# Slot-table fills paced by half head over the attention stage of a bucketed-attention and two-MoE kernel

## The chip, the core and the metric

One core of one Trainium2 chip runs the whole program. The metric is the device time of one execution in microseconds (us); lower is better. Inside the core TensorE (PE in the profile, its weight loads PEld), VectorE (DVE), ScalarE (ACT) and GpSimd (POOL) compute; SyncE (SP) issues most transfers, and sixteen DMA engines carry them. Each engine runs its own instructions strictly in the order in which they stand in its queue, and waits where an instruction waits.

## What is computed

Three layers in a row: attention inside hash buckets, then a mixture of experts with one expert per token, then one with two experts per token. Cut to what matters:

```python
# attention: 2 batches x 8 heads = 16 heads, 768 tokens, 64 columns
q_bucket = bits(q @ proj > 0); k_bucket = bits(k @ proj > 0)      # 6 bits
scores = where(q_bucket == k_bucket, q @ k.T / 8, -1e9)
x = softmax(scores) @ v                                           # -> 1536 tokens x 512
# layer 1: 8 experts, the best one per token
e = argmax(normed(x) @ normed(emb).T / tau)
x = gate * (relu(x @ w1[e]) @ w2[e])
# layer 2: 8 experts, the best two by noisy logits
out[t] = sum over two e: weight * (relu(x[t] @ w1b[e]) @ w2b[e])
```

## The kernel before

**Attention.** The sixteen heads are worked as 32 half heads of 384 query rows. For a half head TensorE makes three score tiles, VectorE takes their maxima (line 602), GpSimd turns these into a scale (607, 608), ScalarE takes the exponentials (612), TensorE transposes them (620), ScalarE and VectorE split each transposed tile in a high and a low part (624, 630), and TensorE multiplies both by `v` (647, 648). Ahead of a head stands its preparation: ScalarE copies the loaded queries and keys to `hx` (line 500), GpSimd makes the remainder `lx` (544), and six transfers by SyncE put rows of both into the score operands: four from `hx` (line 508: `qa`, `ka`, `qb`, `kb`) and two from `lx` (548). These six are called a head's copies below. `hx` and `lx` have two buffers each, so `hx` of a head can be written only when the copies that read `hx` two heads earlier have landed; `qa` and `ka` have two as well, so a head's copies wait until the scores of the head two before it are done. Two more transfers per head load queries, keys and values (392, 393).

**Slot tables.** Both expert layers pass tokens through tables in DRAM: `xs1` and `xs2` have a region for every expert, to which indirect transfers by GpSimd scatter token rows (line 719 for the first layer, in four sets of three, after half heads 14, 15, 30 and 31). Slots that get no token must read as empty, and the output, to which the second layer adds, must start at zero. So the kernel fills 256 rows per expert of `xs1`, 416 of `xs2`, and all of `out`, from one constant row in SBUF, `zrow`. A fill (line 454) writes 16 rows for each of the 8 experts; there are 16 fills of `xs1`, 12 of `out` and 26 of `xs2`. With the load of the noise and the gate weights in front they make the list `inits`, 55 steps, issued in that order on SyncE:

```python
d = t.rearrange("(e r) d -> e r d", e=E)[:, :cap].rearrange("e (j m) d -> j e m d", j=16)
nc.sync.dma_start(d[:, :, k], zrow[0:128:8, None, :rw].to_broadcast([16, E, rw]))
```

**What sets the order.** Every step of the attention stage is entered in a planner (`plan.add`) with its engine, an assumed length, a due time and the steps that it depends on. The planner runs through an assumed clock and writes down in which order each engine gets its instructions. A dependency named there shapes only this order; the waits on the chip follow from the data. The step `("ex", g, 0)` is the first exponential of half head `g`; `("wr", c)` loads a weight tile of the first expert (line 202), the first four of which are split by ScalarE and GpSimd in 32 pieces during attention (lines 211, 217); `("ra", T0, t)` is a scatter of line 719; `x0_load` (731) reads the first expert's slots back after the second set of scatters; `r1_keep` (773) stores finished rows to `xd`.

**Waits of SyncE.** All transfers of SyncE share eight completion semaphores in turn, so each of them waits until the eighth before it has landed. It never has more than eight in flight.

**Afterwards** two expert stages follow, of eight experts each, mainly matrix products on TensorE.

Of the kernel before, what the change touches and what calls it, by code (L numbers as in the profile page):

```python
# [46 lines left out]
BSE = lambda h: BSK if BSA <= h < BSB else 0  # L47
RA, K8, L1, L2 = 0, 7, 20, 1
WP, WR, WS = 4, 30, 2.5
LATE, ZP, Z2, L6, CR = 1, 23.0, 214.0, -4, 12  # L50
XD = 178
XZ, XSB = 13, 2
# [3 lines left out]
class Plan:  # L56
# [7 lines left out]
    def add(self, name, eng, dur, fn, due, deps=(), use=(), new=(), lat=0):  # L64
        self.steps[name] = (eng, dur, fn, due, tuple(deps), tuple(use) + tuple(new), tuple(new), lat)
# [66 lines left out]
def lsh_attention_moe_moe2_kernel(  # L132
# [120 lines left out]
    def rank_carry(pool, oh, T, key):  # L253
        a = pool.tile([128, E], F32R, name="carry", bufs=2)
        nc.gpsimd.tensor_tensor(a, carry[key], oh[:, 0], op=OP.add)
        for t in range(1, T):
            nc.gpsimd.tensor_tensor(a, a, oh[:, t], op=OP.add)
        carry[key] = a
# [43 lines left out]
    def gate1_norm(pool, ss, T, r):  # L302
        nr = r["nr"] = pool.tile([128, T], F32, name="nr")
        nc.gpsimd.tensor_tensor(nr, ss[:, :, 0], ss[:, :, 1], op=OP.add)
        nc.gpsimd.tensor_tensor(nr, nr, half.to_broadcast([128, T]), op=OP.pow)
        nc.gpsimd.tensor_scalar(nr, nr, 1e-6, None, op0=OP.add)

    def gate1_scale(T, r):
        nc.vector.reciprocal(r["nr"], r["nr"])
        nc.vector.tensor_tensor(r["z"], r["z"], r["nr"][:, :, None].to_broadcast([128, T, E]), op=OP.mult)  # L310

    def gate1_exp(r):
        nc.scalar.activation(r["z"], r["z"], AF.Exp)

    def gate1_out(pool, T, r, gate):
        den = pool.tile([128, T], F32, name="den")
        nc.vector.tensor_reduce(den, r["z"], axis=AX.X, op=OP.add)
        nc.vector.tensor_scalar(den, den, 1e-9, None, op0=OP.add)
        nc.vector.reciprocal(gate, den)
# [131 lines left out]
    def init_x(t, rw, k, cap):  # L451

        d = t.rearrange("(e r) d -> e r d", e=E)[:, :cap].rearrange("e (j m) d -> j e m d", j=16)
        nc.sync.dma_start(d[:, :, k], zrow[0:128:8, None, :rw].to_broadcast([16, E, rw]))
# [39 lines left out]
    inits = [init_a] + [lambda k=k: init_x(xs1, RW1, k, CAP1) for k in range(16)] + \  # L494
# [284 lines left out]
    add = plan.add  # L779
    P = lambda f, *a, **k: (lambda: f(*a, **k))  # L780
# [66 lines left out]
    for g in range(NG):  # L847
        h = g // 2
        z = 6.0 * g
        for j in range(3):  # L850
            k, o = (g, j), 2 * j
# [8 lines left out]
        for kb in range(6):  # L860
            k = (g, kb)
# [21 lines left out]
        add(("fo", g), "DVE", 363, P(fin_out, g), z + PR["fin"], [("fp", g), ("fr", g)],  # L883
            use=[("ET", ("f", g)), ("sm", g)])
    for k, f in enumerate(inits):
        add(("in", k), "SP", 900, f, 24 + 2.2 * k, [("in", k - 1)] if k else [("c3",), ("hc", 1)], lat=3000)
    add(("wm",), "PE", 3000, P(warm, W0), -99, [], new=[("ET", "wm")])
    for i, (n, d) in enumerate(((WA, ("sc", 0, 1)), (WB, ("sc", 0, 2)), (WC_, ("sc", 1, 0)))):
        if n:
# [9 lines left out]
    add(("en",), "PE", 380, init_en_pe, 3, [("en3",), ("c2",)], new=[("ET", "en")])  # L899
    add(("ene",), "DVE", 350, init_en_out, 4, [("en",), ("so",)], use=[("ET", "en")])  # L900
    for c in range(8):
        add(("wr", c), "SP", 1700, P(wload, c), (WR if c < WP else 150) + c, ([("in", 2)] if c < WP else [("in", len(inits) - 1)]) + ([("wl", c - 4, 7)] if c > 3 else []),
            lat=2500)
    for c in range(4):
        for k in range(8):
# [3 lines left out]
    for i, g in enumerate((14, 15, 30, 31)):  # L909
        T0, z = 3 * i, 6.0 * g + 8.5 + (L1 if i < 2 else 0)  # L910
        zg = z if i < 2 else z + 8 if i == 2 else z + 4
        hot = [("fo", x) for x in range(g % 2 + 16 * (g // 16), g + 1, 2)]
        w = L2 if i < 2 else .1
        prev = [("rc", T0 - 3)] if T0 else []
        for t in range(3):
            add(("rsa", T0, t), "ACT", 560, P(r1_sq, T0, t, 0), z - 3 + w * t, hot[:-1] + ([("rsa", T0, t - 1)] if t else []),
                use=[("rt", T0)] if t else [], new=[] if t else [("rt", T0)])
            add(("rsb", T0, t), "ACT", 240, P(r1_sq, T0, t, 1), z + (w * t if i < 2 else 4), hot + [("rsa", T0, 2)] + [("th", 31, 5)] * (i == 2), use=[("rt", T0)])
        U = dict(use=[("rt", T0)])
        add(("r7", T0), "DVE", 260, P(r1_pre, T0), z - 3, hot[:-1] + [("rsa", T0, 0)], use=[("rt", T0)])  # L920
        add(("rm", T0), "DVE", 760, P(r1_top, T0), 191.5 if i == 2 else z, hot + [("r7", T0)], use=[("rt", T0)])
        add(("rr0", T0), "PE", 120, P(r1_rank0, T0), z - (0 if i < 2 else 1), prev + [("tr", 31, 5)] * (i == 2) + [("c3",), ("rm", T0) if i < 2 else ("fp", g)], new=[("ET", ("k", T0))])
        add(("rr", T0), "PE", 228, P(r1_rank, T0), z, [("rm", T0), ("rr0", T0)], use=[("ET", ("k", T0)), ("rt", T0)])
        add(("rq", T0), "DVE", 452, P(r1_hot, T0), zg, [("rm", T0)] + [("tl", 1, 31, 5)] * (i == 2), **U)
        add(("rp", T0), "DVE", 315, P(r1_pos, T0), zg, [("rr", T0), ("rq", T0)],
            use=[("ET", ("k", T0)), ("rt", T0)])
        add(("rn", T0), "POOL", 1325, P(lambda T0: gate1_norm(rt, R1[T0]["ss"], 3, R1[T0]), T0), zg,
            [("rsb", T0, t) for t in range(3)], **U)
        add(("rv", T0), "DVE", 309, P(lambda T0: gate1_scale(3, R1[T0]), T0), zg, [("rn", T0), ("rm", T0)], **U)
        add(("re", T0), "ACT", 113, P(lambda T0: gate1_exp(R1[T0]), T0), zg, [("rv", T0)], **U)  # L930
        add(("rg", T0), "DVE", 506, P(lambda T0: gate1_out(rt, 3, R1[T0], xrow[:, T0:T0 + 3, D]), T0), zg,
            [("re", T0)] + [("fo", 31)] * (i == 2), **U)
        for t in range(3):
            add(("ra", T0, t), "POOL", 1038, P(r1_scatter, T0, t), z + 1 + w * t, [("rp", T0), ("rg", T0)]
                + ([("ra", T0, t - 1)] if t else []) + [("in", len(inits) - 1)]
                + ([("rn", 9)] if (T0, t) == (6, RA) else []), **U)
        if i < 3:
            add(("rc", T0), "POOL", 699, P(lambda T0: rank_carry(rt, R1[T0]["hot"], 3, 1), T0), z + (0 if i < 3 else 2),
                [("rm", T0), ("rr0", T0)] + prev, **U)
        add(("ro", T0), "POOL", 1064, P(r1_over, T0), z + 9, [("rp", T0), ("ra", 9 if i > 1 else T0, 2)], **U)  # L940
        add(("rk", T0), "SP", 1500, P(r1_keep, T0), z + (3 if i < 3 else 0), hot)
# [357 lines left out]
    add = plan.add  # L1299
# [9 lines left out]
    for n in range(4, 128):  # L1309
        key, c = divmod(n, 8)  # L1310
# [12 lines left out]
    for key in range(2 * E):  # L1323
# [16 lines left out]
        if key == E:  # L1340
            for d in range(4):
                for h in range(2):
                    k, r = 2 * d + h, [x8(d)]
# [41 lines left out]
        t = z + 16 * q  # L1385
# [223 lines left out]
```

## Time and profile before

| | |
|---|---|
| median of 3 runs | 811.01 us (807.99 to 813.76) |
| the profiled execution's own time | 808.55 us |
| its span, first to last instruction | 806.8 us |
| mean granted TensorE clock | 0.991 of full speed |
| TensorE matmul busy over the span | 774.3 us, 96% |
| VectorE, ScalarE, GpSimd busy | 583.6, 479.5, 382.3 us |

The profiled execution is one execution of the program; 1.75 us of its time lie outside its span. Busy shares are means over stages with different limits, so the rows below are by stretches: the attention stage ends near 282 us, and the rest is the two expert stages. A TensorE that is shown busy is not necessarily at its peak.

### The profile page before, as it was taken

Reading aid. Unit: us, or ns where it says so; the run is one execution under the profiler, and the core shown is the slowest. Engines: PE = TensorE matmul, PEld = TensorE weight load, DVE = VectorE, ACT = ScalarE, POOL = GpSimd, SP = SyncE. Lnnn points to the kernel's source line nnn. Section 1 sums busy time; section 2 is a strip of 40 time slices with the busy share of each in tenths; the row PEclk is TensorE's granted clock in tenths of the full one; section 3 lists DMA queues with packets and bytes.
Section 4 is the critical chain, followed back from the end, with each engine's and each line's share of the span. In section 5 each row is a group of like instructions: output and inputs, shape, how many; then the busy total and the mean of one; then the engine's idle time right before and its main releaser. Section 6 shows DMA issues by size and latency. Waiting matters only on the chain. (4 is left out here: it accounts for less than half of the span.)

```text
span 806.8 us, 14991 instructions
## 1 busy us (share of the span) xinstructions
PE 774.3 (96%) x5078; PEld 748.5 (93%) x5078; DVE 583.6 (72%) x1303; ACT 479.5 (59%) x1009; POOL 382.3 (47%) x669
## 2 busy tenths in 40 slices
PE   8999798998999999999999998999999999999995
PEld 6899787987999999999999998999999999999995
DVE  8999778999999868887787756684566475665511
ACT  6997777986888847556575544464353435354310
POOL 6655344557464260433123322108373745648474
PEclk9999989999999999999999999999999999999998
DMA  8999999664322158886677645765786776856332
GB/s 215 290 237 233 244 235 247 208 187 143 112 67 53 46 178 252 258 255 196 207 231 218 214 161 176 183 192 93 195 172 173 171 182 132 177 147 118 85 35 80
DMA packets 94076, 141.16 MB, mean 175 GB/s; under 512 B 26220, under 2 KB 58116, under 8 KB 93994
## 3 DMA queue, kind: packets, MB, share of 16 engines
q1 hardware_dynamic: 76730, 123.45, 55.2%
q0 software_dynamic: 17264, 16.70, 11.1%
q8 instruction: 42, 0.69, 0.4%
q14 instruction: 40, 0.33, 0.1%
HBM read 89.08 MB, written 36.06 MB: 155 GB/s over the span
## 5 line engine op out<-in xcount | busy, mean ns | idle before, releaser
L1264 POOL DMA_INDIRECT out_dram<-yo,idx x91 | 147.6, 1622 | 127.6 <-DVE yo L1261 102.0
L1056 PE MATMUL S<-xh,w0h 128*128 128x256 f32 (+1 forms) x512 | 165.0, 322 | 1.0 <-DVE hl L1066 1.0
L1057 PE MATMUL S<-xl,w0h 128*128 128x256 f32 (+1 forms) x512 | 161.4, 315 | 0.3 <-issue 0.3
L1058 PE MATMUL S<-xh,w0l 128*128 128x256 f32 (+1 forms) x512 | 161.7, 316 | 0.0
L1080 PE MATMUL ET<-hh,w1h 128*128 128x256 f32 (+2 forms) x504 | 158.5, 315 | 0.1
L1082 PE MATMUL ET<-hh,w1l 128*128 128x256 f32 (+2 forms) x504 | 158.2, 314 | 0.0
L1081 PE MATMUL ET<-hl,w1h 128*128 128x256 f32 (+2 forms) x504 | 157.8, 313 | 0.0
L1062 ACT ACTIVATE hh<-S 128x512 fp32r<-128x512 f32 (+1 forms) x64 | 46.8, 732 | 136.1 <-PE S L1058 130.1
L630 DVE TENSOR_TENSOR el<-ET,eh 128x384 fp32r<-128x384 f32 x192 | 102.0, 551 | 16.1 <-ACT eh L624 13.9
L612 ACT ACTIVATE es<-S,mxs 128x768 f32<-128x768 f32 x96 | 95.5, 995 | 15.7 <-POOL mxs L608 12.8
L620 PE MATMUL ET<-idf,es 128*128 128x128 f32 x576 | 92.1, 277 | 9.7 <-ACT es L612 7.1
L1066 DVE SCALAR_TENSOR_TENSOR hl<-S,hh 128x512 fp32r<-128x512 f32 (+1 forms) x64 | 54.5, 852 | 64.2 <-ACT hh L1062 62.3
L624 ACT ACTIVATE eh<-ET 128x384 fp32r<-128x384 f32 x192 | 89.7, 492 | 14.6 <-PE ET L620 11.3
L1056 PEld LDWEIGHTS S<-xh,w0h 128*128 128x128 f32 x512 | 96.3, 188 | 1.4 <-DVE hl L1066 1.2
L1057 PEld LDWEIGHTS S<-xl,w0h 128*128 128x128 f32 x512 | 96.4, 188 | 1.3 <-issue 0.5
L1058 PEld LDWEIGHTS S<-xh,w0l 128*128 128x128 f32 x512 | 96.2, 188 | 0.3
L1080 PEld LDWEIGHTS ET<-hh,w1h 128*128 128x128 f32 x504 | 94.9, 188 | 1.1 <-ACT ys L1104 0.7
L1081 PEld LDWEIGHTS ET<-hl,w1h 128*128 128x128 f32 x504 | 94.8, 188 | 0.7
L602 DVE TENSOR_REDUCE mxs<-S 128x1 f32<-128x768 f32 x96 | 91.5, 953 | 5.1 <-PE S L597 4.0
L1082 PEld LDWEIGHTS ET<-hh,w1l 128*128 128x128 f32 x504 | 94.7, 188 | 0.3
L620 PEld LDWEIGHTS ET<-idf,es 128*128 128x128 f32 x576 | 71.9, 142 | 20.6 <-ACT es L612 8.1
L217 DVE TENSOR_TENSOR w1l<-wraw,w1h 128x512 fp32r<-128x512 f32 x128 | 81.9, 681 | 11.8 <-ACT w1h L211 11.8
(257 smaller groups left out, 1474.7 us busy)
## 6 DMA issues: line engine op xcount, KB each, us to landing
wraw<-in_w1a_dram SPq DMA_DIRECT2D x32, 512.0 KB
wraw<-in_w2a_dram SPq DMA_DIRECT2D x32, 512.0 KB
wraw<-in_w1b_dram SPq DMA_DIRECT2D x32, 512.0 KB
wraw<-in_w2b_dram SPq DMA_DIRECT2D x32, 512.0 KB
xs<-zrow SPq DMA_DIRECT2D x26, 260.5 KB
xr<-xs SPq DMA_DIRECT2D x28, 208.0 KB
qk<-in_qk_dram SPq DMA_DIRECT2D x15, 384.0 KB
xs<-zrow SPq DMA_DIRECT2D x16, 261.0 KB
```

Source lines behind the costliest of these rows:

```text
L602: nc.vector.tensor_reduce(MX[(3 * g + j) % 9][:, 0:1], SC[g, j][:, :, :384], axis=AX.XY, op=OP.max, negate=True)
L612: nc.scalar.activation(ES[g, j].rearrange("p (a b) -> p a b", a=2), SC[g, j][:, :, :384], AF.Exp, bias=mx[:, 2:3], scale=mx[:, 1:2], accum ...
L620: nc.tensor.transpose(T[:, j * 128:j * 128 + 128], ES[g, j][:, kb * 128:kb * 128 + 128], idf)
L624: nc.scalar.activation(EH[g, kb], ET[g, kb], AF.Copy)
L630: nc.vector.tensor_tensor(EL[g, kb], ET[g, kb], EH[g, kb], op=OP.subtract)
L1056: nc.tensor.matmul(o, wH[n][:, fs], xh, start=kd == 0, stop=False)
L1057: nc.tensor.matmul(o, wH[n][:, fs], xl, start=False, stop=False)
L1058: nc.tensor.matmul(o, wL[n][:, fs], xh, start=False, stop=kd == 3)
L1080: nc.tensor.matmul(P, wH[n][:, ws], hh, start=f == 0, stop=False)
L1081: nc.tensor.matmul(P, wH[n][:, ws], hl_, start=False, stop=False)
L1082: nc.tensor.matmul(P, wL[n][:, ws], hh, start=False, stop=f == 7)
L1264: s = nc.gpsimd.indirect_dma_start(out=out.rearrange("n (a c) -> (n a) c", a=4), out_offset=bass.IndirectOffsetOnAxis(ap=IDX[e][:, b:b + 1 ...
```

## The change

The fills get later due times and, each, a dependency on a half head: step `k` of the list (`FILL` = 0.5) may stand, in the planner's clock, only after the first exponential of half head 3 + k/2. Two followers that named the end of the whole list as a dependency now name an earlier member: the scatters to `xs1` the last fill of `xs1`, the weight loads 4 to 7 member 34. No fill is added, dropped or changed in shape. One constant takes a line of its own, so every line number after line 49 is higher by one.

```diff
 WP, WR, WS = 4, 30, 2.5
+FILL = .5
 LATE, ZP, Z2, L6, CR = 1, 23.0, 214.0, -4, 12
...
     for k, f in enumerate(inits):
-        add(("in", k), "SP", 900, f, 24 + 2.2 * k, [("in", k - 1)] if k else [("c3",), ("hc", 1)], lat=3000)
+        add(("in", k), "SP", 900, f, 24 + 3 * k, [("in", k - 1), ("ex", int(3 + FILL * k), 0)] if k else [("c3",), ("hc", 1)], lat=3000)
...
     for c in range(8):
-        add(("wr", c), "SP", 1700, P(wload, c), (WR if c < WP else 150) + c, ([("in", 2)] if c < WP else [("in", len(inits) - 1)]) + ([("wl", c - 4, 7)] if c > 3 else []),
+        add(("wr", c), "SP", 1700, P(wload, c), (WR if c < WP else 150) + c, ([("in", 2)] if c < WP else [("in", 34)]) + ([("wl", c - 4, 7)] if c > 3 else []),
             lat=2500)
...
             add(("ra", T0, t), "POOL", 1038, P(r1_scatter, T0, t), z + 1 + w * t, [("rp", T0), ("rg", T0)]
-                + ([("ra", T0, t - 1)] if t else []) + [("in", len(inits) - 1)]
+                + ([("ra", T0, t - 1)] if t else []) + [("in", 16)]
                 + ([("rn", 9)] if (T0, t) == (6, RA) else []), **U)
```

Three places in SyncE's queue show what moves. Heads are counted from 0; `qa0`/`ka0` belong to even heads, `qa1`/`ka1` to odd ones, and the numbers after other names are buffer numbers.

First, SyncE from the copies of head 6 to the first copy of head 7. Before:

```order
L508 DMA qa0_139<-hx_1061 64x768
L508 DMA ka0_140<-hx_1061 64x768
L508 DMA qb_1433<-hx_1061 64x768
L508 DMA kb_1434<-hx_1061 64x768
L548 DMA qb_1433<-lx_1079 64x768
L548 DMA kb_1434<-lx_1079 64x768
L392 DMA qk_1510<-in_qk_dram 128x768
L393 DMA vr_1511<-in_v_dram 128x384
L454 DMA xs2_59<-zrow_149 16x8x521 x10
L508 DMA qa1_142<-hx_1346 64x768
```

and of the changed kernel, at the same place:

```order
L509 DMA qa0_139<-hx_1038 64x768
L509 DMA ka0_140<-hx_1038 64x768
L509 DMA qb_1416<-hx_1038 64x768
L509 DMA kb_1417<-hx_1038 64x768
L549 DMA qb_1416<-lx_1055 64x768
L549 DMA kb_1417<-lx_1055 64x768
L393 DMA qk_1490<-in_qk_dram 128x768
L394 DMA vr_1491<-in_v_dram 128x384
L455 DMA xs1_58<-zrow_149 16x8x522 x3
L455 DMA out_0_dram<-zrow_149 16x8x512
L509 DMA qa1_142<-hx_1303 64x768
```

Ten fills between two heads' copies have become four. Before, 9, 10, 9, 10 and 9 fills stand between the copies of neighbouring heads from head 3 to head 8, then 1, then none; now 2, 6, 4, 4, 4 and 4 stand there from head 3 to head 9, then 4, 3, 4, 5, 4 and 4 up to head 15, and 5 after that head.

Second, SyncE ahead of the copies of head 12, before:

```order
L508 DMA qb_2727<-hx_2354 64x768
L508 DMA kb_2728<-hx_2354 64x768
L548 DMA qb_2727<-lx_2368 64x768
L548 DMA kb_2728<-lx_2368 64x768
L392 DMA qk_2800<-in_qk_dram 128x768
L393 DMA vr_2801<-in_v_dram 128x384
L508 DMA qa0_139<-hx_2612 64x768
```

and of the changed kernel:

```order
L549 DMA qb_2718<-lx_2338 64x768
L549 DMA kb_2719<-lx_2338 64x768
L455 DMA xs2_59<-zrow_149 16x8x521
L393 DMA qk_2807<-in_qk_dram 128x768
L394 DMA vr_2808<-in_v_dram 128x384
L455 DMA xs2_59<-zrow_149 16x8x521 x2
L203 DMA wraw_2873<-in_w2a_dram 128x1024
L203 DMA wraw_2903<-in_w2a_dram 128x1024
L203 DMA wraw_2943<-in_w2a_dram 128x1024
L455 DMA xs2_59<-zrow_149 16x8x521
L509 DMA qa0_139<-hx_2587 64x768
```

Four fills and three weight loads (5 to 7 of the eight; the last stands one head later) have come in between the loads and the next copies. Before, these weight loads stood after the last fill, between the copies of heads 8 and 10.

Third, SyncE where the first four weight loads stand. Before, ahead of head 3:

```order
L392 DMA qk_469<-in_qk_dram 128x768
L393 DMA vr_470<-in_v_dram 128x384
L454 DMA xs1_58<-zrow_149 16x8x522
L202 DMA wraw_519<-in_w1a_dram 128x1024
L202 DMA wraw_550<-in_w1a_dram 128x1024
L454 DMA xs1_58<-zrow_149 16x8x522
L202 DMA wraw_599<-in_w1a_dram 128x1024
L454 DMA xs1_58<-zrow_149 16x8x522 x2
L508 DMA qa1_142<-hx_446 64x768
```

and of the changed kernel, ahead of head 4:

```order
L393 DMA qk_705<-in_qk_dram 128x768
L394 DMA vr_706<-in_v_dram 128x384
L455 DMA xs1_58<-zrow_149 16x8x522
L203 DMA wraw_747<-in_w1a_dram 128x1024
L203 DMA wraw_774<-in_w1a_dram 128x1024
L203 DMA wraw_803<-in_w1a_dram 128x1024
L455 DMA xs1_58<-zrow_149 16x8x522
L203 DMA wraw_850<-in_w1a_dram 128x1024
L509 DMA qa0_139<-hx_549 64x768
```

The weight loads, and with them the pieces of their split on ScalarE and GpSimd, come about one head later and with two fills beside them where there were four. On the computing engines the steps of a head keep their places relative to each other but for neighbours that change places; from the first load of the expert stage on, SyncE's queue is the same in both.

## Rows read from the trace of the kernel before

**Rows 1.** Waits over 56 to 140 us: engine, line, what ended them; total, times, longest.

```profile
POOL lx L544 <- DMA kb<-lx: 13.9, 4, 6.0
ACT hx L500 <- DMA kb<-hx: 10.0, 3, 4.9
...
PE ET L620 <- ACT es L612: 6.8, 3, 3.8
...
ACT hx L500 <- DMA qb<-lx: 2.4, 1, 2.4
```

**Rows 2.** Windows cut where each head's copies start; last columns clock, DMA share, GB/s.

```profile
22.30:37.60 15.30, 15.06 (x102) 13.73 (x100) 14.52 (x29) 14.27 (x33) 9.20 (x26) 1.00 0.94 289
37.60:53.80 16.20, 15.95 (x111) 15.04 (x110) 15.72 (x33) 14.89 (x36) 9.88 (x28) 1.00 0.93 240
53.80:72.70 18.90, 18.62 (x127) 17.55 (x127) 18.05 (x37) 16.47 (x40) 10.74 (x31) 1.00 0.99 234
72.70:90.50 17.80, 16.46 (x112) 15.47 (x111) 16.05 (x33) 14.73 (x35) 8.99 (x28) 1.00 0.97 234
90.50:110.10 19.60, 15.79 (x91) 15.06 (x90) 13.25 (x26) 11.97 (x28) 7.64 (x22) 0.83 0.97 230
110.10:127.80 17.70, 15.32 (x100) 13.59 (x99) 14.83 (x29) 13.45 (x31) 8.41 (x25) 1.00 0.98 238
127.80:142.30 14.50, 12.44 (x84) 11.47 (x82) 11.59 (x21) 10.48 (x26) 5.50 (x18) 1.00 0.95 271
142.30:158.00 15.70, 15.45 (x104) 14.35 (x103) 15.12 (x32) 15.11 (x39) 7.18 (x21) 1.00 0.68 209
158.00:173.60 15.60, 15.53 (x104) 14.06 (x102) 15.24 (x42) 14.71 (x42) 8.77 (x24) 1.00 0.57 165
173.60:191.10 17.50, 15.60 (x103) 14.24 (x102) 16.68 (x51) 12.25 (x27) 12.04 (x34) 1.00 0.50 149
191.10:209.60 18.50, 17.43 (x115) 15.36 (x113) 16.97 (x37) 14.44 (x31) 11.08 (x29) 1.00 0.55 168
209.60:225.20 15.60, 15.25 (x104) 14.31 (x102) 15.12 (x30) 13.41 (x29) 7.65 (x22) 1.00 0.30 77
225.20:240.20 15.00, 15.00 (x104) 14.41 (x103) 14.41 (x30) 13.57 (x30) 9.33 (x24) 1.00 0.32 80
```

**Rows 3.** Timeline of SyncE's queue: start, length, line, transfer, count.

```profile
97.37 12.58 SPq L454 DMA_DIRECT2D xs<-zrow  x10
110.07 1.27 SPq L508 DMA_DIRECT2D qa<-hx  x1
...
146.78 0.39 SPq L393 DMA_DIRECT2D vr<-in_v_dram  x1
```

**Rows 4.** Timeline of ScalarE, the copy to hx in a crowded and a free head.

```profile
98.58 0.84 ACT L500 ACTIVATE hx<-qk 128x768 fp32r<-128x768 f32 x1 [4.91 <-DMA kb<-hx]
...
151.78 0.86 ACT L500 ACTIVATE hx<-qk 128x768 fp32r<-128x768 f32 x1
```

**Rows 5.** Timeline of TensorE, the first transpose after its longest wait.

```profile
100.45 0.47 PE L620 MATMUL ET<-idf,es 128*128 128x128 f32 x1 [3.81 <-ACT es L612]
```

**Rows 6.** Windows of 2 us around that wait; columns as in rows 2.

```profile
98.00:100.00 2.00, 0.00 (x0) 0.00 (x0) 0.00 (x0) 1.42 (x2) 0.00 (x0) 0.87 1.00 279
...
102.00:104.00 2.00, 2.00 (x9) 1.81 (x9) 1.77 (x3) 0.95 (x2) 1.89 (x5) 0.50 0.97 213
```

**Rows 7.** Window of the expert stages; columns as in rows 2.

```profile
282.00:807.00 525.00, 510.81 (x3387) 505.37 (x3385) 330.03 (x741) 248.09 (x478) 235.51 (x256) 0.99 0.66 172
```

**Rows 8.** DMA issues by group: transfer, queue, count, size of one.

```profile
xs<-zrow SPq DMA_DIRECT2D x26, 260.5 KB
```

**Rows 9.** Waits of SyncE's queue over 20 to 240 us.

```profile
SPq L508 <- PE S L597: 72.0, 10, 12.5
...
SPq L393 <- POOL mxs L608: 1.4, 5, 0.4
...
SPq L393 <- POOL lx L544: 1.0, 1, 1.0
```

## The prediction

> **What bounds the kernel now.** I read the windows first, cut where each head's copies start. In the second half of the attention stage a head takes 15.0 to 15.7 us and TensorE is busy in nearly all of it; from head 4 to head 8 a head takes 17.7 to 19.6 us, the DMA share is 0.97 to 0.99, and TensorE is idle up to 3.8 us in a window [rows 2]. The waits of that stretch say who stands: ScalarE waits 10.0 and 2.4 us, in four places, at the copy to `hx`, for copies of an earlier head to land; GpSimd waits 13.9 us for `kb<-lx`; TensorE waits 6.8 us behind the exponentials that ScalarE has queued behind that copy [rows 1]. The two heads of 17.5 and 18.5 us later on are the ones with routing and scatters; there the DMA share is 0.50 and 0.55, so their excess is no matter of transfers [rows 2].
>
> Why the copies land late is seen on SyncE: ten fills in a row take it 12.58 us, and the first copy of the next head follows directly, at 110.07 [rows 3]. No compute wait is shown ahead of that copy; SyncE stood behind its own fills. So in this stretch a head lasts as long as its transfers. That can be checked. A fill costs 12.58 / 10 = 1.26 us [rows 3]. The six copies of a head cost 0.30 x 15.6 = 4.7 us of all sixteen engines, from a head with nothing else beside them [rows 2]. The loads of a head I take as the rest of the crowded windows: 0.99 x 18.9 - 4.7 - 12.6 = 1.4, 0.97 x 17.8 - 4.7 - 11.3 = 1.3, 0.97 x 19.6 - 4.7 - 12.6 = 1.7; mean 1.5 [rows 2, 3]. A head with n fills then needs 6.2 + 1.26 n: 18.8 us for ten (18.9 and 19.6 in the rows) and 17.5 for nine (17.8 and 17.7) [rows 2]. The first head with nine fills took only 16.2, since its copies had started ahead of need.
>
> **The free head.** Five heads have neither crowding nor routing: 15.3, 15.7, 15.6, 15.6 and 15.0, mean 15.4 us [rows 2]. A head becomes longer than that when 6.2 + 1.26 n passes 15.4, at n = 7.3. The kernel before has 9 or 10 there; the changed one has 2 to 6 in every head.
>
> **What the change removes.** The six windows from 37.6 to 142.3 last 104.7 us [rows 2]; six free heads are 6 x 15.4 = 92.4. The difference, 12.3 us, is what the fills cost now. [...] It is close to the 12.4 us that ScalarE waits [rows 1]. When the stall goes, TensorE is late next, with 15.25 of 15.6 us busy in a free head, VectorE just behind with 15.12 [rows 2]; the free heads already run at that pace, so nothing further is won.
>
> **What it adds, head by head** (fills counted in the order, costs as above). Heads 4 to 5 now get 6 fills: 6.2 + 7.6 = 13.8 us. Those with 4: 11.2. With a store of `xd` beside them: window 158.0 is 0.57 x 15.6 = 8.9, less 6.2 gives 2.7 for the store [rows 2], so 13.9 with 4 fills and 12.7 with 3. Heads 13 and 14 have no loads: 4.7 + 5.0 = 9.7. All lie under 15.4, and the fills stand behind the loads in a time when SyncE would have waited for scores anyway (72.0 us in ten waits) [rows 9], so I cost these at nothing; the cover is that wait.
>
> Three heads come near the limit. Ahead of head 4 stand four weight loads and 2 fills. A weight load costs what is left of window 142.3: 0.68 x 15.7 = 10.7, less 6.2 and a store of 2.7, 1.8 us [rows 2]. So 6.2 + 2.5 + 7.2 = 15.9, which is 0.5 over. Between heads 11 and 12, which took 17.5, the row holds 0.50 x 17.5 = 8.8 with loads and scatters [rows 2]; 4 fills and 3 weight loads make it 8.8 + 5.0 + 5.4 = 19.2, 1.7 over. Between heads 12 and 13: 0.55 x 18.5 = 10.2, with 5 fills and a weight load 18.3, just under 18.5. What is over doesn't stop ScalarE at once: in a free head the next copy to `hx` starts 151.78 - 142.30 = 9.5 us after the head's copies, which need 4.7, so 4.8 us are spare [rows 2, 4]. The cost of the crowding that is left thus lies between 0 (absorbed) and 2.2 us (all of it felt), or 5 us more if a wait in these heads grows to the one that lets the clock fall: the 3.3 us of clock and a few of standing [rows 2, 5]. I take 1.2, between the first two, as the spare time is more than twice the excess.
>
> The followers: the scatters to `xs1` now wait for its last fill, which stands ahead of head 8, long before the first scatter (after half head 14); nothing. Weight loads 5 to 8 come four heads later but are used only in the expert stage; nothing. The split of weights 1 to 4 moves by one head with the same 32 pieces on ScalarE and GpSimd; bounds -1 to +1, value 0. The last five fills fall after head 15's copies, when DMA is nearly idle, and end well before the expert stage, whose queue is the same; its 525 us [rows 7] are taken over whole.
>
> **Sum.** 12.3 - 1.2 = 11 us less. From the profiled execution's 808.55 (span 806.8 and 1.75 around it) that gives 797.5. That execution lies 2.5 us below the median of the runs shown; from the median, 811.0 - 11 = **800 us**, which I predict.
>
> [...] The rows give 1.26 us a fill of 260.5 KB [rows 3, 8]. [...]
>
> **Rivals.**
> *The heads with weight splits are slower by themselves.* Splits sit on ScalarE in heads 2 to 10, and the window from 37.6, with splits and little harm from fills, took 16.2 us, not 15.4 [rows 2]. If that is their own pace, the four long heads fall to 16.2 only: 18.9 + 17.8 + 19.6 + 17.7 = 74.0 becomes 64.8, and the short head after them, 14.5, which caught up, goes back to 15.7: 9.2 - 1.2 = 8.0; with the 1.2 left over, 6.8 gained, 804. Against it: 15.3 in the window from 22.3, 15.7 in that from 142.3, both with splits. Chance 0.17.
>
> *Crowding comes back in heads 4, 11 and 12*, with a wait of ScalarE and a fall of the clock as at 98 us. Two such places at some 3 us each cost 6: 12.3 - 6 = 6, 805. For it: the two sums at or above the head's length; against it, the spare 4.8 us. Chance 0.12.
>
> *It doesn't do what it says, or the pace is set elsewhere*: only the planner's clock ties fills to half heads, and SyncE is free to issue a head's four at once. If the waits at `hx` were only shown there and heads 4 to 8 stayed long for another reason, nothing moves: 811. Against it: the sums for nine and ten fills. Chance 0.05.
>
> *Slower*: the fills stand behind the loads in SyncE's queue, and a load waits for its buffer. If that wait grows, the fills slip towards the next head's copies and their 5 us go ahead of these, in all heads from 4 on, also the late ones that are free now. In a free head SyncE has issued copies and loads after 146.78 + 0.39 - 142.3 = 4.9 us [rows 2, 3] and needs 5.0 more for four fills, so 15.4 - 9.9 = 5.5 us of wait are harmless, and with the spare 4.8 of ScalarE it decides from some 10 us on. A wait 2 us past that costs 2 us in ten heads: 811 - 12 + 20 = 819. Today the loads wait 0.4 us at most for GpSimd's scales, 1.0 for the remainder [rows 9]. Chance 0.06.
>
> **How the numbers follow.** The forecast, 797 to 803, has the remaining 0.60. About 8 us (1%) is what a measurement of this kernel can tell from no change; the border is 802.9. Faster by over 1%: 0.59 of the forecast and about a fifth of the first two rivals, 0.65. Slower: the last rival, 0.06. Within: 0.29. The range must leave out at most 0.2: on top the slower case and most of the null, below the chance that early heads gain from lighter queues as well; 796 to 808.
>
> **What would show it.** Right: in windows cut at the copies, heads 4 to 8 at 15 to 16 us, no ScalarE wait for `kb<-hx` of over 1 us, the clock at 1.00 between 80 and 140 us, bursts of at most six fills on SyncE, and the attention stage about 11 us shorter with the same 525 us behind it. Wrong: a wait at `hx` around heads 4, 12 or 13 (second rival), no such waits but long heads 4 to 8 (first, third), or long loads ahead of fills (last).

## The result and the profile after

The changed kernel takes 802.76 us, the median of four runs (801.23 to 803.71), beside 810.8 us for the kernel before in the same session (807.99 to 813.76): a ratio of 0.9894, 95% interval 0.9864 to 0.9924. It is 8 us or 1.1% faster, where 11 us were forecast. The profiled execution took 803.71 us, its span is 802.0. Line numbers of the changed kernel are one higher.

Windows of the changed kernel, cut where each head's copies start, from head 3 (38.16) to head 14; the columns are those of [rows 2]:

```profile
38.16:53.58 15.42, 15.01 (x104) 14.33 (x102) 14.84 (x28) 13.11 (x29) 6.78 (x20) 1.00 0.91 277
53.58:69.28 15.70, 15.23 (x104) 14.30 (x102) 15.18 (x31) 14.55 (x37) 10.45 (x30) 1.00 0.88 226
69.28:84.90 15.62, 15.15 (x104) 14.29 (x102) 15.10 (x30) 14.47 (x37) 10.40 (x29) 1.00 0.67 183
84.90:100.51 15.61, 15.21 (x104) 14.31 (x102) 15.09 (x30) 13.93 (x33) 8.65 (x25) 1.00 0.67 183
100.51:116.12 15.61, 15.19 (x104) 14.28 (x102) 15.10 (x31) 13.98 (x33) 8.65 (x25) 1.00 0.70 182
116.12:131.72 15.60, 15.18 (x104) 14.28 (x102) 15.10 (x30) 13.89 (x32) 7.25 (x22) 1.00 0.67 182
131.72:147.78 16.06, 15.44 (x104) 14.15 (x103) 15.47 (x38) 15.32 (x39) 7.05 (x21) 1.00 0.78 226
147.78:164.31 16.53, 15.99 (x109) 14.66 (x107) 16.12 (x43) 14.23 (x40) 10.16 (x31) 1.00 0.72 205
164.31:180.63 16.32, 14.69 (x96) 13.21 (x94) 14.44 (x41) 12.17 (x28) 11.19 (x30) 1.00 0.91 254
180.63:201.33 20.70, 19.84 (x117) 18.85 (x116) 18.43 (x41) 13.88 (x31) 11.18 (x30) 0.84 0.94 292
201.33:216.75 15.42, 15.01 (x104) 14.31 (x102) 14.85 (x30) 13.48 (x29) 7.25 (x20) 1.00 0.65 149
```

The six windows from head 3 to head 9 last 131.72 - 38.16 = 93.6 us against 104.7 in [rows 2]; TensorE idles at most 0.5 us in one, and the DMA share falls from 0.97 to 0.67 once the weight loads are through. The four from head 9 to head 13 go the other way, 69.6 against 67.3, with the last at a clock of 0.84. Of these 2.3 us, 1.3 lie in the first two (32.6 against 31.3) and 1.0 in the last two (37.0 against 36.0). The 20.70 by itself misleads: the head before it takes 16.32 where it took 17.5, because steps of the routing now stand in other windows (96 and 117 instructions of TensorE in these two, 103 and 115 before).

Three of the waits over those crowded heads (53.58 to 131.72), as in [rows 1]. No transfer is left anywhere in that list; ScalarE's copy to `hx` waits 0.6 us in all, for TensorE:

```profile
PE ET L621 <- DVE el L631: 2.2, 5, 0.5
POOL lx L545 <- ACT hx L501: 1.2, 3, 0.4
...
ACT hx L501 <- PE ET L568: 0.6, 3, 0.2
```

SyncE's queue between two heads, as in [rows 3], and its first wait over 20 to 240 us, as in [rows 9]. After four fills the queue is free from 78.5 to 84.9, and the next head's copies start when the scores let them:

```profile
73.74 0.39 SPq L394 DMA_DIRECT2D vr<-in_v_dram  x1
74.17 4.34 SPq L455 DMA_DIRECT2D xs<-zrow  x4
84.90 0.50 SPq L509 DMA_DIRECT2D qa<-hx  x1
```

```profile
SPq L509 <- PE S L598: 74.6, 14, 11.4
```

Two stretches gave time back. In the window of 20.70 us the granted clock is 0.50 of full speed for some 7 us (182.9 to 189.7), behind a string of short idle stretches of TensorE (2.5 of 14 us between 170 and 184); two rows of 2 us, as in [rows 6]:

```profile
184.00:186.00 2.00, 2.00 (x11) 2.00 (x11) 1.85 (x6) 1.08 (x2) 1.36 (x4) 0.50 1.04 251
186.00:188.00 2.00, 2.00 (x10) 1.90 (x9) 1.60 (x4) 0.98 (x2) 1.61 (x4) 0.50 1.00 308
```

And from the first read of the slots (line 997) to the end the changed kernel takes 514.9 us, the profiled one before 511.4; the row answers to [rows 7]:

```profile
287.13:802.00 514.87, 498.81 (x3275) 492.92 (x3273) 318.78 (x705) 239.99 (x458) 223.43 (x239) 0.99 0.66 171
```

So within the profiled pair attention ends 8.25 us earlier (287.13 for 295.38) and 3.5 of them are lost again. The experiments ask three things: is it the volume of fills in a head that made these heads long; what makes the four heads with routing longer, transfers or the order of the steps; and is the loss behind attention real.

### The profile page after: what moved, and what is told of

Its sections match the earlier page's. It is cut to its first block, busy times and chain, and to the rows that moved or that the text cites. A ratio compares the mean times of both kernels' runs of the same rounds, so it can differ in the third digit from the quotient of the medians.

```text
span 802.0 us, 14985 instructions
## 1 busy us (share of the span) xinstructions
PE 772.9 (96%) x5078; PEld 749.3 (93%) x5078; DVE 583.4 (73%) x1303; ACT 480.0 (60%) x1009; POOL 381.0 (48%) x669
## 6 DMA issues: line engine op xcount, KB each, us to landing
xs<-zrow SPq DMA_DIRECT2D x26, 260.5 KB, 5.0
```

## Experiments

Three lengths are read from every run: head 3 to head 9 (the six windows), head 9 to head 13 (the four with routing), each from copies to copies, and from the first read of the slots to the end.

| kernel | heads 3-9 | heads 9-13 | read to end | median us (ratio) |
|---|---|---|---|---|
| before, first and second profile | 104.7, 103.1 | 67.3, 67.4 | 511.4, 513.4 | 810.17 of 17 runs |
| changed, first and second | 93.6, 92.7 | 69.6, 68.6 | 514.9, 514.6 | 802.76, 801.32 (0.9883) |
| before, late fills taken out | 93.0 | 67.0 | | 847.01 (one run, 38 fills behind the stage) |
| changed, late fills taken out | 93.6 | 68.4 | | 853.83 (one run, the same) |
| changed, weight loads moved | 92.7 | 68.6 | 516.5 | 802.12 (0.9888) |
| changed, three per half head | 92.6 | 68.4 | 513.0 | 802.02 (0.9892) |
| pacing alone, 4 a head, twice | 92.6, 93.0 | 67.1, 67.0 | 515.0, 515.3 | 799.59 (0.9871), 799.65 (0.9857) |
| pacing alone, 5 a head | 93.2 | 67.1 | 516.7 | 799.86 (0.9865) |
| pacing alone, 8 a head | 97.3 | 71.4 | 516.7 | 809.63 (0.9988) |
| 4 a head, a later read | 93.0 | 67.1 | 513.8 | 799.35 (0.9868) |
| before, fills on GpSimd | 106.9 | 67.2 | 515.7 | 817.46 (one run) |

**Late fills taken out, order kept (e1 of the kernel before, e2 of the changed one).** The planner keeps its steps, so no engine's order moves; the 38 fills of `out` and `xs2` are issued behind the stage.

```diff
+    late, inits = inits[17:], inits[:17] + [lambda: None] * 38
     for k, f in enumerate(inits):
...
     att.close()
+    for f in late:
+        f()
```

> The kernel before, with the 38 fills of out and xs2 taken out of the attention stage and issued in one block behind it; the 16 fills of xs1 stay where they were, and every other instruction of the attention stage keeps its place on its engine. The total is not to be read: the block stands ahead of the first read-back and should cost some 38 x 1.26 = 48 us. To be read are the windows cut at the copies. Theory (transfers set the pace of the crowded heads): heads 4 to 8 fall from 17.7-19.6 us to 15.4-15.7 with no wait of ScalarE for kb<-hx over 1 us, with the order of the kernel before; only the head with nine fills of xs1 (ahead of head 4) may be longer, 16.2 as before. Rival 1 (weight splits slow these heads by themselves): they stay at 16.2 or more. Rival 3 (pace set elsewhere): 17.7 to 19.6 stay. The two heads with routing (17.5 and 18.5) had no fills and should not move.

> The same done to the changed kernel: fills of out and xs2 behind the attention stage, the order of all computing engines that of the changed kernel. Total not to be read (some 48 us more). To be read: the two heads with routing, 16.5 and 20.7 us in the changed kernel, the second at a clock of 0.84. If the fills and weight loads beside them cost the time there (crowding), the second falls to 18.5 or less, at a clock of 1.00, since its DMA share falls from near 1 to near 0.5. If the changed order of the routing steps is the cause, it stays near 20.7 with the clock at half for some 6 us. The other heads: 15.4 to 15.7 in either case; if the remaining fills cost something in the free heads, they fall below the 15.6 of the changed kernel.

The windows of e1, heads 4 to 9, columns as above:

```profile
53.31:67.73 14.42, 14.32 (x98) 13.63 (x97) 13.82 (x27) 12.43 (x30) 8.04 (x23) 1.00 0.71 179
67.73:83.86 16.13, 15.47 (x104) 14.22 (x103) 15.50 (x32) 14.17 (x33) 8.29 (x25) 1.00 0.41 112
83.86:99.28 15.42, 15.00 (x104) 14.29 (x102) 14.84 (x28) 14.01 (x34) 8.96 (x25) 1.00 0.43 115
99.28:114.76 15.48, 15.36 (x104) 14.25 (x103) 14.97 (x32) 13.83 (x32) 7.89 (x24) 1.00 0.43 116
114.76:130.19 15.43, 15.01 (x104) 14.30 (x102) 14.82 (x28) 13.92 (x33) 8.05 (x24) 1.00 0.71 218
```

With the order of before and no late fills, the long heads are gone: 93.0 us for the six. It is the fills, and the first rival (weight splits) and the third (pace set elsewhere) fall: the splits are all still there. e2 gives 93.6 for the changed kernel without late fills, the same as with them, so paced fills cost nothing there. In its last two routing heads:

```profile
163.72:180.04 16.32, 14.71 (x96) 13.23 (x94) 14.46 (x41) 12.17 (x28) 11.20 (x30) 1.00 0.83 254
180.04:199.54 19.50, 17.51 (x117) 15.77 (x116) 18.07 (x41) 13.80 (x31) 11.08 (x30) 1.00 0.63 187
```

Of the 20.70 us, 1.20 went, with the clock back at 1.00. The 19.50 that stay are no loss: with the 16.32 ahead of them they make 35.8 us, against 36.0 in [rows 2]. What is longer in e2 stands before that, from head 9 to head 11, where neither a fill nor a weight load is left:

```profile
131.14:147.19 16.05, 15.45 (x104) 14.20 (x103) 15.46 (x38) 15.33 (x39) 7.04 (x21) 1.00 0.55 161
147.19:163.72 16.53, 15.99 (x109) 14.67 (x107) 16.12 (x43) 14.23 (x40) 10.17 (x31) 1.00 0.54 156
```

Together they take 32.6 us, against 31.3 in [rows 2], so it is not the moved fills and weight loads that cost time there. The order of the steps is what is left; e6 below tests it.

**Weight loads out of the routing heads (e3), three fills per half head (e4).**

```diff
-... else [("in", 34)]) + ([("wl", c - 4, 7)] if c > 3 else []),
+... else [("in", 24)]) + ([("wl", c - 4, 7)] if c > 3 else []),
```

> The changed kernel with weight loads 5 to 8 tied to member 24 of the list in place of 34: three of them stand between heads 9 and 10 and one between 10 and 11, out of the routing heads; nothing else moves on any engine. If the weight loads crowd the routing heads: that pair of heads falls from 16.5 and 20.7 by the 3 us of clock, total 2 to 4 us less than the changed kernel (ratio to before 0.985). If the order of the routing steps is the cause: 16.5 and 20.7 as in the changed kernel, total the same, 0.989.

```profile
179.40:199.11 19.71, 18.87 (x117) 17.26 (x116) 18.31 (x41) 14.14 (x31) 11.29 (x30) 0.91 0.76 227
```

The DMA share of the window falls from 0.94 to 0.76; its length is that of the second profile of the changed kernel, 19.66 with a DMA share of 0.92 (below). The weight loads cost nothing there; the whole time is the changed kernel's.

> The changed kernel with three fills per half head (FILL 0.34): 9 fills between the copies of heads 4 and 5, 6 each in the three heads after, then 6 with two weight loads, 4 with two, 8, 4 and 1. By the sum 6.2 + 1.26 n, six fills make 13.8 us and stay under the 15.6 of a free head: those heads at 15.4 to 15.7. The one with nine makes 17.5 on its own, but the copies have 4.8 us to spare, so between 15.6 (absorbed) and 17.5. Six fills with two weight loads: 6.2 + 7.6 + 3.6 = 17.4, and eight fills 16.3: these are near the limit and cost 0 to 2.5 together. Heads with routing have fewer fills than in the changed kernel. Total 0 to 4 us above the changed kernel if crowding is felt above n = 7.3, the same or a little less if the spare time takes it up.

```diff
-WP, WR, WS, FILL = 4, 30, 2.5, .5
+WP, WR, WS, FILL = 4, 30, 2.5, .34
```

The head with nine fills and the one behind it:

```profile
54.29:70.49 16.20, 15.73 (x109) 14.80 (x108) 15.49 (x32) 15.11 (x40) 10.98 (x32) 1.00 0.93 235
70.49:84.90 14.41, 14.39 (x99) 13.70 (x98) 13.82 (x27) 13.38 (x34) 9.45 (x26) 1.00 0.99 248
```

Together 30.6, two free heads: a single head over the limit, 17.5 by the sum, is taken up whole, since its copies are late by less than ScalarE has to spare. Heads with six fills take 15.6.

**The kernel before once more (e5) and the changed one (e9).**

> The kernel before, unchanged, for a second profile of it. The changed kernel gave back some 4 us in the expert stages (from the read of the first expert's slots to the end: 511.4 us before, 514.9 after, and 516.5 and 513.0 in the two timed experiments). If that is a change of one execution to another, this one shows 512 to 516 as well; if the expert stages are slower because attention ends sooner, it stays near 511. The six crowded windows should again take 104 to 105 us.

> The changed kernel once more, timed beside the run with pacing alone, for a second profile. Attention: head pair with routing (heads 8 to 12) 68.4 to 69.7 us against 67.1 to 67.4 in the order of the kernel before; from the first read of the slots to the end 513 to 517 us, as in six other executions with and without the change (511.4 to 516.7), so that what the expert stages gave back in the first profile was the difference of two executions. Median 802 to 803.

(The stretch meant in the second text is from head 9 to head 13.) From the read of the slots to the end, e5, then the last two of these heads in e9:

```profile
293.41:806.80 513.39, 497.91 (x3278) 491.84 (x3276) 318.61 (x705) 240.36 (x458) 225.21 (x241) 0.99 0.66 172
```

```profile
162.95:179.28 16.33, 14.71 (x96) 13.24 (x94) 14.45 (x41) 12.20 (x28) 11.22 (x30) 1.00 0.90 251
179.28:198.94 19.66, 18.87 (x117) 17.25 (x116) 18.29 (x41) 14.10 (x30) 11.31 (x30) 0.91 0.92 300
```

With 513.4 us in the same kernel, e5 lies 2 us above the first profile of before and inside the 513.0 to 516.7 of the others, as expected of a change from one execution to another. e9 shows that the 20.70 was partly chance: the same kernel takes 19.66 with the clock at 0.91, and the last two heads together 36.0 us. The six windows of before were 103.1 this time, below the 104 expected, and the median of e9, 801.32, lies below the 802 expected.

**Pacing alone (e6, e10: four a head; e7: five; e8: eight).** The order of the planner is that of the kernel before, and only the fills from the sixth on are put elsewhere, a fixed number ahead of each head's copies from head 4 on. Every computing engine has the order of before, row for row.

```diff
-    for f in plan.order():
-        f()
+    plan.order()
+    names = [n for _, _, n in sorted(plan.starts)]
+    rest = [n for n in names if n[0] == "in" and n[1] > 5]
+    for n in [n for n in names if n not in rest]:
+        if n[0] == "hc" and len(n) == 2 and n[1] > 3:
+            for m in rest[:4]:
+                plan.steps[m][2]()
+            rest = rest[4:]
+        plan.steps[n][2]()
+    for m in rest:
+        plan.steps[m][2]()
```

> Pacing alone: the order of every computing engine, and of loads, weight loads and copies, is that of the kernel before; only the fills from the sixth on are moved, four ahead of each head's copies from head 4 on. If the pacing is all that gains, and the changed places of the routing steps cost 1 to 2 us: heads 4 to 8 at 15.4 to 15.7 as in the kernel without late fills (six windows 93.0), heads 9 to 12 as before (31.3 and 36.0 us for the two pairs, against 32.6 and 37.0 in the changed kernel), and the total 1 to 3 us below the changed kernel, ratio 0.986. If the order of the other engines was part of the gain: 802 or more.

> Pacing alone with four fills a head (as e6), timed beside the changed kernel on one chip. If the changed order of the routing steps costs the 1 to 2 us that the windows show: 1 to 3 us below the changed kernel, near 800; else the same.

> As the run before with five fills ahead of each head: 6.2 + 6.3 = 12.5 us for a head, under 15.6, with three weight loads 17.9 in one head, which the spare 4.8 us of the copies takes up. One head fewer gets fills, and none stands late in the stage. Same time as four per head, within 1 us; if the place of the fills in the routing heads costs anything, up to 2 us less.

From head 11 to head 13, in e6 and then in e10, which is the same kernel:

```profile
161.37:179.25 17.88, 15.98 (x102) 14.66 (x101) 17.02 (x53) 12.22 (x27) 12.04 (x34) 0.96 0.72 205
179.25:197.38 18.13, 17.71 (x115) 16.48 (x114) 16.87 (x35) 14.52 (x31) 11.11 (x29) 0.95 0.77 231
```

```profile
162.92:180.42 17.50, 15.61 (x103) 14.28 (x102) 16.67 (x51) 12.22 (x27) 12.03 (x34) 1.00 0.74 209
180.42:198.91 18.49, 17.45 (x115) 15.37 (x113) 16.98 (x37) 14.43 (x31) 11.07 (x29) 1.00 0.78 227
```

As expected: 92.6 and 93.0 for the six windows, and the four heads with routing at the 67.3 of before, with four fills in each of them. In this order fills cost nothing there either, so what the changed kernel pays there is its order: 68.4 to 68.6 with the clock little disturbed, some 1.2 us, and once 69.6. The loss is from head 9 to head 11; there e6 has, against the two windows of e2 above:

```profile
130.30:146.02 15.72, 15.64 (x106) 14.61 (x105) 15.20 (x33) 15.02 (x38) 7.38 (x22) 1.00 0.86 243
146.02:161.37 15.35, 15.29 (x103) 13.79 (x101) 14.99 (x42) 14.46 (x42) 8.78 (x24) 1.00 0.97 268
```

These take 31.1 us, less than the 32.6 of e2, although the DMA share is 0.86 and 0.97 and in e2 0.55 and 0.54. VectorE (the third busy time) is nearly full in both, with 30.2 of 31.1 us in e6 and 31.6 of 32.6 in e2. The changed order has put 1.4 us more work of VectorE into these heads: steps of the routing stand earlier. It shows on TensorE too: its first rank product (line 241, in the changed kernel 242) starts at 176.69 before, 3.1 us behind the start of head 11's copies, and in the changed kernel at 159.97, 4.3 us ahead of it. So these are more than neighbours changing places. From head 11 to head 13, which that work has left, VectorE has time to spare and nothing is won: 35.8 to 36.1 us in e2, e3 and e9, and 36.0 in e6 and e10.

What TensorE waits for over the four heads fits. In e2 it waits 0.6 us for the gate's denominator ahead of a rank product, and twice some 0.5 us for the low parts from VectorE; e6, in the order of before, shows none of these, and waits 0.2 us for the one-hot rows:

```profile
PE ET L241 <- DVE den L317: 0.6, 1, 0.6
PE ET L620 <- DVE el L630: 1.1, 2, 0.6
```

```profile
PE ET L249 <- DVE hot L290: 0.2, 1, 0.2
```

The first two make 1.7 us; TensorE is idle for 4.7 us of these four heads in e2 and for 3.1 in e10, both at a clock of 1.00. That the order is the cause is shown by e2, e3 and e6; that it acts through a full VectorE is read off these rows, and no run moved the routing steps alone. Four timings of the changed kernel's order (802.76, 802.12, 802.02, 801.32) all lie above the three of pacing alone with four or five fills (799.59, 799.65, 799.86); each single comparison lies within its interval. Five a head does the same as four.

> As the two before with eight fills ahead of each of five heads, then eight with three weight loads: 6.2 + 1.26 x 8 = 16.3 us a head against 15.4 to 15.6 free. By that sum each of five heads is 0.7 to 0.9 over, 4 us, and the sixth, with 21.7, some 6 over; the spare 4.8 us of the copies takes up what comes first, so 3 to 6 us more than with four per head. If a burst costs nothing until ten (no break-even at 7.3), the same time as four per head; if every burst over four costs, as much as the kernel before, 8 us more.

SyncE ahead of head 8 in e8, and the windows from head 5 to head 10:

```profile
109.07 9.86 SPq L454 DMA_DIRECT2D xs<-zrow  x8
119.04 1.29 SPq L508 DMA_DIRECT2D qa<-hx  x1
```

```profile
69.97:85.94 15.97, 15.38 (x104) 14.22 (x103) 15.37 (x32) 13.71 (x32) 8.32 (x25) 1.00 1.00 244
85.94:101.57 15.63, 15.21 (x104) 14.31 (x103) 15.05 (x29) 14.20 (x34) 9.14 (x26) 1.00 1.00 246
101.57:119.04 17.47, 17.18 (x115) 15.63 (x115) 16.93 (x35) 15.14 (x35) 9.23 (x27) 1.00 0.96 230
119.04:136.38 17.34, 16.61 (x110) 15.37 (x110) 15.66 (x31) 14.84 (x35) 8.25 (x26) 1.00 0.97 287
136.38:156.27 19.89, 14.57 (x86) 13.72 (x85) 12.86 (x26) 12.36 (x31) 5.43 (x17) 0.83 0.85 221
```

ScalarE's longest wait in that stretch:

```profile
ACT hx L500 <- DMA kb<-hx: 6.0, 1, 6.0
```

The DMA share is 1.00 and yet the first heads take 15.6 to 16.0: each runs a little over and eats into the spare time of the copies. Once that is gone, heads take 17.3 and 17.5, and behind the head with three weight loads ScalarE stands 6.0 us at `hx` and the clock goes, as at 98 us before [rows 4 to 6]. From head 3 to head 10 it is 117.2 us against 108.3 in e6: 8.9 more, of which an estimated (1 - 0.83) x 19.89 = 3.4 is clock; the other 5.5 lie in the 3 to 6 expected, and the clock was missing there. The median is 10.0 us above four a head, as much as if every burst over four cost; the windows speak against that reading, since the first heads are hardly longer. Eight fills a head give the whole gain back: 0.9988.

**A later read (e11).** The kernel of e6; in the planner the read of expert 2's slots depends on the sixth weight load of expert 1 too, and comes behind its second half.

```diff
-... ([("xl", key - 1)] if key else [("go",)])
+... ([("xl", key - 1)] + [("wr", 13)] * (key == 2) if key else [("go",)])
```

> Pacing alone with four fills a head, and the read of expert 2's slots moved behind the second half of expert 1's weights. In the first expert stages TensorE waits for expert 1's weights, whose transfers share the engines with that read. If this is what stretches them, the wait of ScalarE for them shrinks and the total falls by 1 to 3 us; if the weights wait for the slots' read-back alone, no change; a few DVE and ScalarE steps change places, which may cost up to 1 us.

No change: 799.35 us, against 799.65 for the same kernel without the move. From 283 to 340 us ScalarE waits 3.5 us for expert weights (`w0h`, line 211), against 5.3 in e10; one profile of each, and the total does not follow.

**Fills on GpSimd's queue (e12).**

```diff
-        nc.sync.dma_start(d[:, :, k], zrow[0:128:8, None, :rw].to_broadcast([16, E, rw]))
+        nc.gpsimd.dma_start(d[:, :, k], zrow[0:128:8, None, :rw].to_broadcast([16, E, rw]))
```

> The kernel before with its fills issued by GpSimd in place of SyncE, at the same times of the plan: nine or ten a head are still carried, spread between GpSimd's steps of that head, and no copy stands behind a fill in its queue. If the volume sets the pace (6.2 + 1.26 n for a head, all queues sharing the sixteen engines), heads 4 to 8 stay at 17.5 to 19 us and the total near 811. If only the place in SyncE's queue did it, they fall to 15.4-15.7 and the total to about 800. Against a clean reading: a fill that waits on GpSimd holds up the scales, which would show as waits of ScalarE for GpSimd.

Windows from head 4 to head 8, and two of the waits in them:

```profile
55.87:72.70 16.83, 15.73 (x104) 14.24 (x102) 14.95 (x30) 13.60 (x33) 13.52 (x35) 1.00 0.93 244
72.70:89.31 16.61, 15.73 (x104) 14.17 (x103) 15.19 (x32) 14.06 (x34) 12.41 (x33) 1.00 0.94 242
89.31:112.07 22.76, 16.11 (x103) 14.68 (x102) 14.70 (x29) 13.10 (x33) 15.06 (x38) 0.96 0.88 215
112.07:131.06 18.99, 17.95 (x104) 16.42 (x103) 15.42 (x31) 14.10 (x33) 14.29 (x36) 0.86 0.91 227
```

```profile
ACT es L612 <- POOL mxs L608: 14.5, 8, 5.8
...
POOL lx L544 <- DMA qk<-in_qk_dram: 5.9, 2, 5.0
```

Out of SyncE's way, nine to eleven fills a head (9, 9, 11 and 10 in these windows) still make the four heads 75.2 us, 18.8 each, where the sum has 73.9: what is won in the first two is paid in the third, where GpSimd waits 5.0 us for a head's queries and keys that come late, and ScalarE for the scales behind it. That fits the volume setting the pace, with the queue only picking who waits: the DMA share is 0.88 to 0.94 in all four. But the waits for GpSimd keep this from being a clean measure, so it is not shown by this run alone.

## Why the prediction was right, and where it was off

**The bound and the gain: right.** Heads 4 to 8 were as long as their transfers. The term was 104.7 less six heads of 15.4, 12.3 us; the two profiles of each kernel give 104.7 and 103.1 less 93.6 and 92.7, on average 10.8. Of the 1.5 missing, 0.8 is the second profile of before, shorter than the first, and the rest free heads of 15.4 to 15.7 in place of 15.4. That the fills cause it is shown by e1, and that their number over several heads decides, by e8.

**The sum 6.2 + 1.26 n: right as an average, too strict for one head.** Eight fills passed the limit, five and six did not; but the limit bites only when the 4.8 us to spare are used up, after four heads of eight, and not at all for a single nine. The prediction's own check of the sum was weaker than it looks: the 1.5 us for a head's loads were what is left of three crowded windows, so these three had to come out near it, and only the 17.7 of the fourth was a test. The runs check it from outside. By the DMA share a head without fills takes 0.43 x 15.45 = 6.6 us of all engines (e1, against 6.2), one with four fills 0.67 x 15.6 = 10.5 (the changed kernel, against 11.2): an estimated 1.0 us a fill where there is room, less than the 1.26 of the burst.

**The cost of a fill: the row held.** In e8 eight fills take SyncE 9.86 us, 1.23 each, and the head that they stand in 17.47. Nor is it only SyncE's transfers beside them that make a fill cost this: in e1 the first seven fills of `xs2` behind the stage, with no other transfer of SyncE among them, take it 9.61 us, 1.37 us each. The row gives 260.5 KB in 1.26 us, some 210 GB/s. More than that has been moved at a like DMA share: in the profile of before, 193 GB/s at 0.97 from 103 to 109 us, where nearly all packets are rows of fills, and 341 at 1.03 from 98.95 to 101.87, where rows of copies and loads stand among them. In the packet records of the same profile a row of a fill (2,084 or 2,088 bytes) takes 80 to 100 ns in three cases of ten and 155 to 180 ns in six, two speeds a factor of two apart. What sets them is not shown by any run.

**Residual crowding, 1.2 us: wrong; it was nothing.** Head 4, 15.9 by the sum, took 15.42. Heads 11 to 13 keep their length without the weight loads (e3) and, but for the clock, without the fills (e2). The fall of the clock there is no sign of crowding either: e1, with no fill and no weight load in these heads, has 0.96 and 0.95. The 3.3 us of clock in the prediction's bounds is an estimate, (1 - 0.83) x 19.6 of [rows 2], and no run shows it; where the clock fell between heads 12 and 13, the window took 20.70 us at 0.84, and 19.50 in e2 at 1.00. The second rival falls with it, and so does the fourth: SyncE's loads never wait over 2.6 us for a buffer, and no head starts late behind fills.

**The order of the computing engines: the step that failed.** The prediction said that what moves on them costs nothing (split move, value 0), and priced no change of places in the four heads with routing; what stands ahead of it speaks of neighbours only. There the changed order costs 1.1 to 1.3 us, between heads 9 and 11, and 2.3 in the one profile where the clock fell further. It stands where 1.2 us of crowding was put in, so the sum hid the mistake, by luck.

**The expert stages, taken over whole: right as far as the runs go.** The first pair gave back 3.5 us. But twelve profiles, all but one (e11) with the same order in these stages, range from 511.4 to 516.7, and e8, whose attention ends as late as that of before, stands at the upper end. For before the median of 810.17, less 1.7 outside the span and 294.4 (the mean of two profiles) to the read, leaves 514.1; pacing alone leaves 799.62 - 1.7 - 284.0 = 513.9. Both profiled executions of before were 1.7 us under its median. A difference of a microsecond or two is not excluded.

**The size.** In the profiles attention ends 8.5 us earlier (means of two: 294.4 and 285.9), as the medians say (8.0, and 8.1 below 809.4 in the session of e9): 10.8 less some 1.8 in the four heads with routing and 0.5 elsewhere. Pacing alone, with 799.6, is where the forecast of 800 lay.

## What to carry to other kernels

In this kernel background transfers cost nothing while what is carried in one turn of the loop fits its length (92.6 to 93.2 us for the six heads with four or five fills each, 93.0 without late fills), and spare time in front of a buffer takes up a single turn that doesn't (92.6 with one of nine); what counts is the sum over a few turns (97.3 with eight in each), not the longest burst. When a planner moves such transfers, compare the order of the other engines as well: here 1 to 2 of 11 us went there, and putting the same transfers into the old order kept it. Where steps have moved from one turn to another, windows must be added up over several turns before they are compared. One profile against another can mislead by several microseconds in a stage that the change never touched (here 511.4 against 514.9 us, with 513.4 in a second profile of the kernel before).

## What the runs showed of the hardware

The clock is not a property of the order alone: two executions of one kernel (e6, e10) had 0.96 and 0.95, and 1.00 and 1.00, from head 11 to head 13, and the pair took 36.0 us in both: TensorE's idle time there, 2.9 us in e10 and 2.3 in e6, took the loss up. In the changed kernel, at 0.84, it cost 1.0 (37.0 against the 36.0 of e9 at 0.91). A fill issued by GpSimd takes 0.57 us of its own time (two in 1.14, 90.18 to 91.32 in e12); in the kernel before all 54 stand in SyncE's queue, for 577 to 1,807 ns each, and none on a computing engine.
